# Where the third load of wo stands in SP's queue: a one-token decode block on one core

## The chip, the core and the metric

One core of a Trainium2 chip runs the kernel alone. The metric is the device time of one launch in microseconds (us). Before the change the median of three runs is 406.3 us (406.21 to 406.33).

## What is computed

One token of width 1024 goes through a layer norm and then through two branches, whose sum is added to the token:

```python
x = A_x                       # [1, 1, 1024], bf16
xn = _layernorm(x)
# branch A: attention over a cache of 65,536 keys, 32 query heads in 4 groups of 8
q = (xn @ wq).reshape(...)    # wq [1024, 4096]
scores = einsum(q, k) * 128 ** -0.5      # k_cache [1, 4, 65536, 128]
o = einsum(softmax(scores), v)           # v_cache [1, 4, 65536, 128]
A = o.reshape(1, 1, 4096) @ wo           # wo [4096, 1024]
# branch B: a two-stage MLP (with one token the shifted parts of h are all zero)
h = gelu(layernorm(xn) @ w1);  x1 = xn + shifted(h) @ w2
B = x1 + gelu(layernorm(x1) @ w3) @ w4   # w4 [3584, 1024]
out = x + A + B
```

Nearly all of the work is reading: keys and values are 64 MiB each, the weights another 34 MiB. Each byte is used once.

## The kernel before

**Slots.** Everything large is read from HBM into `slots_sb`, eight slots of 16 KB for each of the 128 partitions (2 MiB a slot). A load of keys or values takes two neighbouring slots (4 MiB), a load of `wo` one (2 MiB). The table `where` (L301) fixes the slot of each load: the last values go to slots 4 and 5 or 0 and 1 in turn (`where["v", h, j]`, L306), the last keys to 6 and 7 or 2 and 3, the four loads of `wo` to slots 2, 3, 6 and 7, and the three loads of `w4` to slots 4 and 5, then 0, then 1.

**SP's queue.** All these loads are issued by one engine, SP, in the order of the list `loads`. An issue waits, on SP, until the last users of its slot are through; whatever stands behind it on SP waits too, even where its own slot is long free. The lines are L324 (two slots), L318 (one slot: `w1`, `w2`, `wo`) and L339 (the last pieces of `w4`).

**Heads.** For each of four groups of heads the kernel reads four loads of keys, k(4h) to k(4h+3), and four of values, numbered v0 to v15 over the kernel. A load of keys is turned by VectorE (L542), multiplied on TensorE (L555), and its maximum and copy taken (L566, L567). After the fourth, `finish_head` makes the maximum of the head (L574 to L578) and the exponentials (L580, ScalarE); `transpose_p` turns these on TensorE (L589) and copies them back (L592); only then can `use_v` multiply with the values (L603). `combine` (L610 to L622) ends a head. Values run five loads behind keys (`LAG`, L627), so that after the last keys, k15, five loads of values are left: v11 of the third head and v12 to v15 of the fourth. The loads of `wo` are put in between by hand (L632).

**The end.** When v15 is used up and the head combined, the four parts of `wo` are multiplied (`use_wo`, L531, matmuls of L460), then the parts of `w4` (`use_w4`, L525, also L460). Both add into one PSUM tile; L716 adds the rest and L719 writes the output.

**What each of the last loads waits for**, besides its place in SP's queue: v12 (slots 4, 5) for v10, wo0 and wo1 (slots 2, 3) for k14, v13 (slots 0, 1) for v11, v14 (slots 4, 5) for v12, v15 (slots 0, 1) for v13, wo2 and wo3 (slots 6, 7) for k15, the first load of `w4` (slots 4, 5) for v14, the others (slots 0, 1) for v15.

The order of use on TensorE is not the order of the loads: `uses` (L626 to L640) takes keys and values in the order of the list but puts all of `wo` behind v15.

Of the kernel before, what the change touches and what calls it, by code (L numbers as in the profile page):

```python
# [163 lines left out]
def bass_parallel_sum__gqa_block_cached__mixer_s_mlp__decode_kernel(  # L164
# [37 lines left out]
    with ExitStack() as es:  # L202
# [425 lines left out]
        n_kv = 4 * HKV  # L628
        order = [("k", i) for i in range(LAG)]
        for i in range(LAG, n_kv):  # L630
            order += [("v", i - LAG), ("k", i)]
        order += [("v", n_kv - 5), ("v", n_kv - 4), ("wo", 0), ("v", n_kv - 3), ("wo", 1), ("v", n_kv - 2), ("v", n_kv - 1), ("wo", 2), ("wo", 3)]  # L632
        for kind, i in order:
            loads.append((kind,) + divmod(i, 4) if kind != "wo" else (kind, i))
            if kind != "wo":
# [119 lines left out]
```

## Time and profile before

| | |
|---|---|
| median of three runs | 406.3 us (406.21 to 406.33) |
| the profiled execution's own time | 405.76 us |
| its span, first to last instruction | 404.0 us |
| read from HBM | 169.87 MB, 420 GB/s over the span |
| VectorE busy | 183.8 us (45%) |
| TensorE busy | 154.8 us (38%) |
| ScalarE busy | 75.3 us (19%) |

The 16 DMA engines that move the data have no row among the compute engines; the line "DMA" of the slices gives their mean busy share, and "GB/s" what they moved. One slice of 40 is 10.1 us. The last loads are issued at these times (the timeline of SP; "to landing" is from the issue until all 16 engines have delivered, so issue plus this is the time of landing):

| load | issued at | us to landing | landed at |
|---|---|---|---|
| k15 (4 MiB) | 285.88 | 27.6 | 313.5 |
| v11 (4 MiB) | 287.60 | 35.6 | 323.2 |
| v12 (4 MiB) | 309.52 | 23.4 | 332.9 |
| wo0 (2 MiB) | 309.90 | 27.9 | 337.8 |
| v13 (4 MiB) | 332.04 | 15.5 | 347.5 |
| wo1 (2 MiB) | 332.42 | 20.0 | 352.4 |
| v14 (4 MiB) | 351.18 | 12.4 | 363.6 |
| v15 (4 MiB) | 352.93 | 20.5 | 373.4 |
| wo2 (2 MiB) | 353.30 | 24.9 | 378.2 |
| wo3 (2 MiB) | 353.79 | 29.3 | 383.1 |
| w4, first (4 MiB) | 367.80 | 26.2 | 394.0 |
| w4, second (2 MiB) | 375.49 | 23.4 | 398.9 |
| w4, last piece (256 KiB) | 378.05 | 23.4 | 401.5 |

### The profile page before, as it was taken

To read this page: it belongs to the slowest core of one execution; us is meant where nothing else is said; L and a number is where in the kernel's file an instruction comes from. 1 tells how busy PE (TensorE), PEld (TensorE's weight loads), DVE (VectorE), ACT (ScalarE), POOL (GpSimd) and SP (SyncE) were. 2 spreads that over 40 slices of the span, in tenths; PEclk is the share of its full clock that TensorE was granted. 3 is DMA by queue.
4 is the path that set the end of the run, shared out by engine and by line. 5 is a ranking of instruction groups with operands and counts; after the bars stand their busy time and mean duration, and the time that the engine had idled before them with its cause. 6 is when DMAs were issued, how large, how long until landed. Compare 5 with 4: busy or idle time off the path is not lost. (4 is left out here: it accounts for less than half of the span.)

```text
span 404.0 us, 3803 instructions
## 1 busy us (share of the span) xinstructions
PE 154.8 (38%) x1615; PEld 67.8 (17%) x1615; DVE 183.8 (45%) x137; ACT 75.3 (19%) x71; POOL 7.8 (2%) x38
## 2 busy tenths in 40 slices
PE   0165323244257041344561513257215152603705
PEld 0023110011023010111320101123101012301403
DVE  0135019998747263746545364748180931000200
ACT  1000000111762010191310002813010157200000
POOL 6010000000000000000000000000000000000000
PEclk9995565555556756565575565555956555666777
DMA  8999999999999999999999999999999999899995
GB/s 357 422 415 420 458 419 420 455 417 419 443 435 415 441 441 415 435 448 415 422 454 422 419 454 425 419 444 431 419 438 441 415 425 454 334 415 436 441 414 219
DMA packets 6937, 170.00 MB, mean 421 GB/s; under 512 B 904, under 2 KB 912, under 8 KB 1296
## 3 DMA queue, kind: packets, MB, share of 16 engines
q1 hardware_dynamic: 6772, 169.87, 98.3%
q8 instruction: 6, 0.10, 0.1%
q10 hardware_dynamic: 156, 0.01, 0.0%
q14 instruction: 3, 0.02, 0.0%
HBM read 169.87 MB, written 0.00 MB: 420 GB/s over the span
## 5 line engine op out<-in xcount | busy, mean ns | idle before, releaser
L542 DVE STREAM_TRANSPOSE X<-slots_sb 128x4096 f32<-128x4096 f32 x32 | 141.2, 4428 | 84.3 <-DMA slots_sb<-in_A_k_cache_dram 84.3
L555 PE MATMUL S_ps<-X,Ycur 128*32 128x512 bf16 x512 | 57.8, 596 | 139.9 <-PEq L64 126.3
L603 PE MATMUL OT_ps<-slots_sb,pT_sb 128*32 128x512 bf16 x512 | 50.9, 568 | 22.9 <-PEq L64 22.6
L567 ACT ACTIVATE S_sb<-S_ps 128x1024 f32<-128x1024 f32 x16 | 16.4, 1026 | 181.4 <-DVE mcol L566 161.4
L555 PEld LDWEIGHTS S_ps<-X,Ycur 128*32 128x32 bf16 x512 | 16.8, 124 | 176.6 <-issue 160.9
L580 ACT ACTIVATE p_sb<-S_sb,brun 128x1024 bf16<-128x1024 f32 x16 | 40.5, 2580 | 2.5 <-DVE brun L578 2.2
L603 PEld LDWEIGHTS OT_ps<-slots_sb,pT_sb 128*32 128x32 bf16 x512 | 19.9, 132 | 48.6 <-issue 46.0
L611 DVE TENSOR_TENSOR O_m<-OT_ps,selT_f 128x512 f32<-128x512 f32 x4 | 2.8, 691 | 52.1 <-PE OT_ps L603 52.1
L589 PE MATMUL PT_ps<-ident_bf,p_sb 128*128 128x128 bf16 x128 | 16.2, 307 | 18.5 <-PEq L64 18.5
L566 DVE TENSOR_REDUCE mcol<-S_ps 128x1 f32<-128x1024 f32 x16 | 19.1, 1195 | 8.6 <-PE S_ps L555 8.6
L592 ACT ACTIVATE pT_sb<-PT_ps 128x1024 bf16<-128x1024 bf16 x16 | 16.4, 1024 | 34.3 <-PE PT_ps L589 34.3
L589 PEld LDWEIGHTS PT_ps<-ident_bf,p_sb 128*128 128x128 bf16 x128 | 12.4, 138 | 24.2 <-issue 24.2
L460 PE MATMUL S_ps<-slots_sb,xn_bf 128*32 128x512 bf16 (+1 forms) x128 | 12.3, 556 | 10.4 <-DMA slots_sb<-in_B_w_dram 9.0
L460 PE MATMUL M_ps<-slots_sb,gh_bf 128*32 128x256 bf16 x112 | 5.7, 357 | 12.0 <-DMA slots_sb<-in_B_w_dram 12.0
L471 ACT ACTIVATE ge_a<-ge_b 128x8 f32<-128x8 f32 (+1 forms) x2 | 0.4, 217 | 52.2 <-DVE ge_b L470 52.2
L716 DVE TENSOR_TENSOR fin<-accr,M_ps 128x256 bf16<-128x256 f32 x1 | 0.4, 421 | 21.2 <-PE M_ps L460 21.2
L464 DVE STREAM_TRANSPOSE X<-S_ps 128x512 f32<-128x512 f32 (+1 forms) x3 | 2.6, 850 | 14.1 <-PE S_ps L460 14.1
L420 DVE CAST xP<-xP_bf 128x8 f32<-128x8 bf16 x1 | 0.2, 172 | 16.7 <-DMA xr_bf<-in_A_x_dram 16.7
L460 PEld LDWEIGHTS S_ps<-slots_sb,xn_bf 128*32 128x32 bf16 x128 | 4.5, 134 | 16.6 <-DMA slots_sb<-in_B_w_dram 9.8
L622 ACT ACTIVATE oP_bf<-cb_o 128x8 bf16<-128x8 f32 x4 | 0.8, 210 | 33.1 <-DVE cb_o L621 33.1
L460 PEld LDWEIGHTS M_ps<-slots_sb,gh_bf 128*32 128x32 bf16 x112 | 3.5, 123 | 14.2 <-DMA slots_sb<-in_B_w_dram 13.5
L434 PE MATMUL M_ps<-ln_s,ones_f 128*128 128x1 f32 x6 | 1.5, 328 | 10.6 <-DVE ln_s L433 10.6
(88 smaller groups left out, 59.1 us busy)
## 6 DMA issues: line engine op xcount, KB each, us to landing
slots_sb<-in_A_k_cache_dram SPq DMA_DIRECT2D x16, 4096.0 KB, 27.0
slots_sb<-in_A_v_cache_dram SPq DMA_DIRECT2D x16, 4096.0 KB, 26.8
slots_sb<-in_A_wq_dram SPq DMA_DIRECT2D x2, 4096.0 KB, 16.9
slots_sb<-in_A_wo_dram SPq DMA_DIRECT2D x4, 2048.0 KB, 26.4
slots_sb<-in_B_w_dram SPq DMA_DIRECT2D x2, 3584.0 KB, 32.5
slots_sb<-in_B_w_dram SPq DMA_DIRECT2D x3, 2048.0 KB, 25.9
slots_sb<-in_B_w_dram SPq DMA_DIRECT2D x1, 4096.0 KB, 26.2
slots_sb<-in_B_w_dram SPq DMA_DIRECT2D x1, 512.0 KB, 23.0
```

Of the source, the lines that this page charges most:

```text
L434: _op(q_pe, lambda e: e.matmul(M0_ps[:, c0:c0 + 1], ones_f[:, :], ln_s[:, 0:1], start=True, stop=True), reads=[b_ln, b_const], writes=[b_M0])
L460: e.matmul(out_fn(j), st_fn(kk, j), mv_fn(kk, j), start=st, stop=sp, tile_position=(0, 32 * j), skip_group_check=True))
L464: _op(q_dve, lambda e: e.transpose(out=X32[:, 1, c0:c0 + 32 * n], in_=src), reads=b_src, writes=[b_X[1]], partial=c0 > 0)
L542: turn = lambda e: e.transpose(out=X32[:, m, :], in_=K32)
L555: fns.append(lambda e, we=we, c_mid=c_mid, mv=mv: e.matmul(S_ps[bank][32 * c_mid:32 * c_mid + 32, :], Ycur[:, we, :, :].rearrange("p a g - ...
L566: _op(q_dve, lambda e: e.reduce_max(mcol[:, x:x + 1], S2, axis=AX.X), reads=[b_S[2 * i], b_S[2 * i + 1]], writes=[b_mcol], partial=x > 0)
L567: _tell(q_act, lambda e: e.activation(S_sb[:, 2 * x:2 * x + 2, :].rearrange("p s c -> p (s c)"), S2, ACTF.Copy), t_s, reads=[b_S[2 * i], b ...
L580: fn = lambda e, x=x: e.activation(p_sb[:, :, :, :, x], S_sb[:, 2 * x:2 * x + 2, :].rearrange("p s (c i) -> p s c i", i=32), ACTF.Exp, bia ...
L589: _taking(q_pe, [(t_t, 1) if c8 else (t_p, 1)], [lambda e, i=i, c=8 * c8 + i: e.transpose(out=PT_ps[:, i * P:(i + 1) * P], in_=p_sb[:, c / ...
L592: _tell(q_act, lambda e, c8=c8: e.activation(pT_sb[:, :, 32 * c8:32 * c8 + 32, :].rearrange("p a x g -> p x a g"), PT_ps[:, :].rearrange(" ...
L603: fns.append(lambda e, cl=cl, q4=q4, x0=x0: e.matmul(OT_ps[32 * q4:32 * q4 + 32, :], pT_sb[:, a, x0:x0 + 4, :].rearrange("p x g -> p (x g) ...
L611: _op(q_dve, lambda e: e.tensor_tensor(out=O_m[:, :, :], in0=OT_ps[:, :].rearrange("p (t d) -> p t d", t=4), in1=selT_f[:, :].unsqueeze(2) ...
```

## The change

In the hand-written order of the last loads, `("wo", 2)` moves from behind v14 and v15 to in front of them. Nothing is added or removed; slots, the order of use on TensorE and all other loads stay.

```diff
-        order += [("v", n_kv - 5), ("v", n_kv - 4), ("wo", 0), ("v", n_kv - 3), ("wo", 1), ("v", n_kv - 2), ("v", n_kv - 1), ("wo", 2), ("wo", 3)]
+        order += [("v", n_kv - 5), ("v", n_kv - 4), ("wo", 0), ("v", n_kv - 3), ("wo", 1), ("wo", 2), ("v", n_kv - 2), ("v", n_kv - 1), ("wo", 3)]
```

With `n_kv` = 16 the order of SP's issues at the end becomes v11, v12, wo0, v13, wo1, **wo2**, v14, v15, wo3, then the loads of `w4`.

## The prediction

> **What bounds the kernel now.** I read the page's slices and queues first, then the chain that ended last, then the timeline and SP's waits near the end.
>
> ```profile
> DMA  8999999999999999999999999999999999899995
> GB/s 357 422 415 420 458 419 420 455 417 419 443 435 415 441 441 415 435 448 415 422 454 422 419 454 425 419 444 431 419 438 441 415 425 454 334 415 436 441 414 219
> HBM read 169.87 MB, written 0.00 MB: 420 GB/s over the span
> DMA slots_sb<-in_B_w_dram 6%; PE OT_ps L603 1%; SPq L339 0%; DVE fin L716 0%; PE M_ps L460 0%
> ```
>
> The DMA engines are busy in nearly every slice while VectorE, the busiest compute engine, is at 45%. So the kernel is as long as its stream of loads, plus every moment in which the stream stands still. One slice inside stands out: the 35th (343 to 353 us) with 334 GB/s where its neighbours have 415 to 454. The chain ends in the last piece of `w4`. Next, how that slice comes about, from the timeline:
>
> ```profile
> 332.04 0.33 SPq L324 DMA_DIRECT2D slots_sb<-in_A_v_cache_dram  x1
> 332.42 0.43 SPq L318 DMA_DIRECT2D slots_sb<-in_A_wo_dram  x1
> 347.84 4.97 PE L603 MATMUL OT_ps<-slots_sb,pT_sb 128*32 128x512 bf16 x64 [1.36 <-PEq L64]
> 351.18 2.08 SPq L324 DMA_DIRECT2D slots_sb<-in_A_v_cache_dram  x2
> 353.30 0.94 SPq L318 DMA_DIRECT2D slots_sb<-in_A_wo_dram  x2
> SPq L54 <- PE OT_ps L603: 18.3, 1, 18.3
> ```
>
> SP issues v13 and wo1 at 332, then stands 18.3 us (the last line, from SP's waits) until v12 is used up at 351.18. TensorE begins v12 only at 347.84, because the exponentials and their transposes come first (L580, L589, L592, 328.5 to 347.5). Meanwhile the queue holds what v13 and wo1 left, and that is all delivered by 352.4. The windows show it run dry; a packet counts in the window in which it starts:
>
> ```profile
> 349.20:349.80 0.60, 0.60 (x12) 0.24 (x8) 0.00 (x0) 0.00 (x0) 0.00 (x0) 0.50 1.03 437
> 349.80:350.40 0.60, 0.60 (x12) 0.22 (x8) 0.00 (x0) 0.00 (x0) 0.00 (x0) 0.50 0.71 300
> 350.40:351.00 0.60, 0.60 (x16) 0.34 (x12) 0.00 (x0) 0.00 (x0) 0.00 (x0) 0.84 0.39 164
> 351.00:351.60 0.60, 0.60 (x20) 0.29 (x16) 0.00 (x0) 0.00 (x0) 0.00 (x0) 1.00 0.26 109
> 351.60:352.20 0.60, 0.60 (x16) 0.30 (x12) 0.00 (x0) 0.00 (x0) 0.00 (x0) 1.00 0.61 164
> 352.20:352.80 0.60, 0.60 (x12) 0.11 (x4) 0.00 (x0) 0.00 (x0) 0.00 (x0) 1.00 2.31 655
> 352.80:353.40 0.60, 0.01 (x3) 0.00 (x0) 0.00 (x0) 0.00 (x0) 0.00 (x0) 1.00 0.13 55
> 353.40:354.00 0.60, 0.00 (x0) 0.00 (x0) 0.00 (x0) 0.00 (x0) 0.00 (x0) 1.00 0.00 0
> 354.00:354.60 0.60, 0.00 (x0) 0.00 (x0) 0.00 (x0) 0.00 (x0) 0.00 (x0) 1.00 1.93 819
> ```
>
> The last number of a row is GB/s. 437 is 16 packets of 16 KB in 0.6 us, one for each engine. At 350.4 only 6 engines start another (164), at 351.0 only 4 (109): ten engines ran dry near 350.6, six up to 1.4 us later. v14's first packets, of 32 KB, start near 352.3, the second ones after 354. **The pause is real, but not of one length for all 16 engines.** That is the point on which the size hangs.
>
> **The change, part by part.** No instruction is added or removed: four kinds of things could move.
>
> 1. *wo2's own issue.* Slot 6 was last used by k15, whose matmuls of that half end by 320.2 (L555 at 318.26, 1.90 us); v13, ahead on SP, waits for v11's matmuls, later on TensorE. So wo2 adds no wait to SP and is issued right behind wo1, at 332.42 + 0.43, about 332.9 instead of 353.30. The issue itself is a row of 0.43 us, hidden in SP's 18.3 us wait; without that cover it would delay v14 by 0.43.
>
> 2. *The pause.* Landings (issue plus time to landing) tell the stream's pace: v13 lands 9.7 us after wo0 (347.5 - 337.8), wo1 4.9 us after v13. wo2 now keeps the stream fed 4.9 us beyond wo1: to about 355 on the early engines, 357 on the last. v14 stays at 351.18, since TensorE's work up to there touches nothing of wo2, and its first packets came 1.1 us behind its issue (352.3). So the cover is some 3 us too long, and the pause goes wholly. Its price: v14 landed 363.6 - 352.4 = 11.2 us behind wo1 where 9.7 is the pace, so 1.4 us (1.43 with the marks below) for the engine that ends last. The trace also keeps sixteen completion marks a transfer, one for each engine: wo1's lie between 350.61 and 352.45, v14's between 362.87 and 363.60. The earliest engine thus lost 12.26 - 9.72 = 2.54 us. The pause let the early ones wait and the late ones catch up.
>
> 3. *The end.* What the end gains is between these, and turns on which engines end last. In the last rows:
>
> ```profile
> 399.40:400.00 0.60, 0.60 (x24) 0.34 (x15) 0.00 (x0) 0.00 (x0) 0.00 (x0) 1.00 0.21 68
> 400.00:400.60 0.60, 0.39 (x12) 0.12 (x8) 0.00 (x0) 0.00 (x0) 0.00 (x0) 1.00 0.13 41
> q8 instruction: 1, 0.02, 3.3%
> q8 instruction: 1, 0.02, 3.5%
> ```
>
> A share of 0.13 is two engines of 16: the other 14 are done (the last piece's marks: first 399.64, fourteen by 400.3, two at 401.4 to 401.5). The two q8 lines are DMA windows of 384 to 386 and 398 to 400: in each a block of program, 16 KB, was fetched (3.3% of 16 engines over 2 us is 1.06 us on one engine). The first shows in the landings: `w4`'s first load needs 10.9 us behind wo3 (394.0 - 383.1), 1.2 over the pace. The same is how the six late engines of 350 us came about: such fetches (two of 8 KB) at 35, 69, 71, 84, 108 and 253 us, and after each the marks have one more late engine, none of them struck twice.
> Without the pause the first engine's last mark is 399.64 - 2.54 = 397.10. The six stay late to the end, the worst by 1.84: 398.94. An engine that was early and is struck late ends at 401.49 - 2.54 = 398.95 or, with the 0.3 us by which the early ones differ, up to 399.2. So the last landing moves from 401.49 to about 399.05: **2.4 us less**. Bounds: 2.54 less at best; 0.7 where the engine struck is the most belated one (it ends at 397.10 + 1.84 + 1.85, the last being the lateness of the two struck engines, so 400.8). I take the upper part, as the six fetches before the pause struck six different engines and the three behind it three.
> The Trainium skill, "DMA: Bandwidth & Descriptors", section on the anatomy of one DMA, would make a load from an empty queue cost some 2.0 us fixed plus its bytes at 436 GB/s; by that v14 would have landed 11.6 us behind its issue, at 362.8, the pause would have cost the last engine 0.6 in place of 1.4, and an estimate by it is some 0.8 less gain, 404.7. The trace has 12.4 us for the same load, so it disagrees and is used; the page's fit is for GpSimd's path.
>
> 4. *What is late next.* v14 and v15 come behind wo2: v14 lands at 352.4 + 4.9 + 9.7 = 367.1 (was 363.6), v15 at 376.8 (was 373.4). Then come v15's matmuls (3.6), the combination (377.2 to 380.9, 3.7) and `wo`'s products (96 and 32 matmuls, 2.8 + 1.1, the 96 partly beside the combination): done by 386 to 388. The cover is the wait for `w4`'s first load, 9.8 us in the profile (384.2 to 394.0); its landing moves to about 391.5, so 3 us of cover stay. If they did not, each us of lateness would cost one. `w4`'s first issue follows v14's use, 367.80 + 3.5 = 371.3, with v15 and wo3 still in the queue until 381; the pieces of L339 move likewise and stay 10 us ahead of need. No second pause.
>
> Sum: 405.76 - 2.4 = 403.4 for the profiled execution; the runs' median lies 0.5 above it (406.3), so **403.9**.
>
> **The rivals.**
>
> A. *A late fetch strikes an engine already late.* The same pause goes, but one engine ends at 400.06 to 400.8: a gain of 0.7 to 1.4, time 404.9 to 405.6, say 405.2. For it: six of 16 engines are late by then, and two fetches come; were the choice blind, over half of the cases would be so. Against: none was struck twice in either stretch.
>
> B. *It moves the pause, or wo2 is late after all* (the change does not do what it says): a wait of wo2 on something near 351, or the pause coming again at 371 before `w4`. Then 1.4 us is paid as before: 406.3. Against: the slot's users end at 320.2, and 10 us of loads stand queued at 371.
>
> C. *Slower: the pause was what kept the engines together.* With it gone lateness adds up over the whole kernel. If both late fetches strike the one engine that is 1.84 late, at 1.6 us each (1.85 less some earlier lateness), it ends at 397.10 + 1.84 + 3.2 = 402.1, 0.6 us over before: 406.9. It decides once one engine has 4.4 us of fetches on it. For it: lateness from 35 us was still there at 350. Against: fetches have gone to different engines.
>
> **How the numbers follow.** The forecast has 0.66, A 0.22, B 0.07, C 0.05. A measurement tells about 0.2%, 0.8 us, from no change. B falls under that, and the 0.02 of A with a gain under 0.8; so faster 0.66 + 0.20 = 0.86, same 0.09, slower 0.05. The range reaches from the full 2.54 with a little for the runs' spread, 403.4, to A's upper end, 405.6.
>
> **What would show it.** wo2's issue at about 332.9 and no stretch of a microsecond under 350 GB/s between 349 and 356; v14's issue still at 351.2, its landing near 367; the last landing near 399.0 with six or more engines finishing 1 to 2 us behind the rest; `w4`'s first load landing near 391.4; TensorE waiting some 3 us or more for it. Wrong would be a TensorE without that wait, a new SP wait in front of wo2, or an end near 400.5 with a single engine last (A).

## The result and the profile after

The changed kernel takes **403.38 us** (median of four runs, 403.24 to 403.39) where the kernel before takes 406.28 (406.21 to 406.33): a ratio of **0.9931**, 95% interval 0.9919 to 0.9943, or 2.9 us less. The profiled execution has 403.38 us, its span is 401.6 us (before 404.0). Of the 25 runs of the kernel before that stand beside the experiments below, one took 425.23 us, alone in a slow state, and is not compared with any other (the median of 406.19 given below is 406.17 without it).

From the page of the changed kernel, the DMA engines' slices and what was read:

```profile
DMA  8999999999999999999999999999999999999995
GB/s 359 425 416 418 460 428 419 425 455 418 416 431 457 418 418 434 454 418 418 444 444 418 421 454 431 419 428 454 421 421 431 450 410 432 421 460 421 422 414 232
HBM read 169.87 MB, written 0.00 MB: 423 GB/s over the span
```

The bytes are the same. The 35th slice has 421 GB/s instead of 334, and no slice inside stands out any more. SP's issues, from the timeline (start, duration, engine, line, tiles, count):

```profile
331.70 0.33 SPq L324 DMA_DIRECT2D slots_sb<-in_A_v_cache_dram  x1
332.08 0.90 SPq L318 DMA_DIRECT2D slots_sb<-in_A_wo_dram  x2
351.31 2.45 SPq L324 DMA_DIRECT2D slots_sb<-in_A_v_cache_dram  x2
```

Two loads of `wo` now follow v13 at 332, and v14 still goes out only at 351.3. What the DMA engines do meanwhile, in the windows (the last number is GB/s, counted by the start of each packet):

```profile
349.80:350.40 0.60, 0.60 (x12) 0.28 (x8) 0.00 (x0) 0.00 (x0) 0.00 (x0) 0.50 1.03 437
350.40:351.00 0.60, 0.60 (x9) 0.20 (x5) 0.00 (x0) 0.00 (x0) 0.00 (x0) 0.50 0.90 382
351.00:351.60 0.60, 0.60 (x12) 0.35 (x8) 0.00 (x0) 0.00 (x0) 0.00 (x0) 0.50 1.03 437
351.60:352.20 0.60, 0.60 (x16) 0.23 (x8) 0.00 (x0) 0.00 (x0) 0.00 (x0) 0.80 0.90 382
352.20:352.80 0.60, 0.60 (x20) 0.32 (x12) 0.00 (x0) 0.00 (x0) 0.00 (x0) 1.00 1.02 437
352.80:353.40 0.60, 0.52 (x12) 0.02 (x4) 0.00 (x0) 0.00 (x0) 0.00 (x0) 1.00 1.03 437
353.40:354.00 0.60, 0.00 (x0) 0.00 (x0) 0.00 (x0) 0.00 (x0) 0.00 (x0) 1.00 0.90 382
```

382 and 437 are 14 and 16 packets of 16 KB in 0.6 us: all engines go on without a break, where before they went from 300 down to 109 between 349.8 and 351.6. The end, in the same view:

```profile
396.40:397.00 0.60, 0.54 (x12) 0.44 (x16) 0.00 (x0) 0.00 (x0) 0.00 (x0) 0.50 0.81 297
397.00:397.60 0.60, 0.60 (x20) 0.44 (x16) 0.00 (x0) 0.00 (x0) 0.00 (x0) 0.50 0.50 181
397.60:398.20 0.60, 0.60 (x20) 0.44 (x16) 0.00 (x0) 0.00 (x0) 0.00 (x0) 0.50 0.39 143
398.20:398.80 0.60, 0.60 (x16) 0.24 (x8) 0.00 (x0) 0.00 (x0) 0.00 (x0) 0.50 0.06 20
```

A DMA share of 0.50 and 0.39 is about half of the 16 engines, in a stretch in which the others are done. Before, it was two engines of 16 that came last. The marks of the last piece say the same: before, fourteen lie between 399.64 and 400.4 and two at 401.4 to 401.5; now seven lie between 397.14 and 397.4 and nine between 397.7 and 398.99. The last landing moved from 401.49 to 398.99 us, by 2.50. The span became only 2.38 shorter, because the last four products, behind that landing, took 0.29 us before (granted clock 1.00 in that window) and 0.41 now (0.50).

### The profile page after: what moved, and what is told of

It reads as the page before. It is cut to its first block, busy times and chain, and to the rows that moved or that the text cites. A ratio compares the mean times of both kernels' runs of the same rounds, so it can differ in the third digit from the quotient of the medians.

```text
span 401.6 us, 3803 instructions
## 1 busy us (share of the span) xinstructions
PE 151.8 (38%) x1615; PEld 65.7 (16%) x1615; DVE 183.7 (46%) x137; ACT 75.3 (19%) x71; POOL 7.7 (2%) x38
## 5 line engine op out<-in xcount | busy, mean ns | idle before, releaser
L589 PE MATMUL PT_ps<-ident_bf,p_sb 128*128 128x128 bf16 x128 | 14.8, 287 | 19.0 <-PEq L64 19.0
L589 PEld LDWEIGHTS PT_ps<-ident_bf,p_sb 128*128 128x128 bf16 x128 | 11.2, 129 | 24.2 <-issue 24.2
L615 PE MATMUL M_ps<-O_L,selL 128*128 128x129 f32 x8 | 2.8, 444 | 8.1 <-PEq L64 8.1
```

Of the source, the lines that this page charges most:

```text
L589: _taking(q_pe, [(t_t, 1) if c8 else (t_p, 1)], [lambda e, i=i, c=8 * c8 + i: e.transpose(out=PT_ps[:, i * P:(i + 1) * P], in_=p_sb[:, c / ...
L615: _taking(q_pe, [(t_o, 1)], [lambda e: e.matmul(M0_ps[:, 256:257 + P], selL[:, :, :].rearrange("p g x -> p (g x)"), O_L[:, :], start=True, ...
```

## The experiments

Times are medians; the kernel before was run beside each group of kernels on the same chip (406.19 beside the first, 406.15 beside the second). "Lateness" is by how much a completion mark of a transfer lies behind the first of its sixteen marks. The marks carry no name of an engine; which mark belongs to the same engine in the next transfer is read from the distances, which hardly change from one transfer to the next.

### The kernel before, a second profile

No edit.

> The kernel before, unchanged, for a second profile. The theory (the pause near 350 us has a price that depends on how late each DMA engine is, and blocks of program fetched by a DMA engine make it late): the same pause, issue of v14 near 351, v14 landing some 11.2 us behind wo1; a span between 404.0 and 404.6, since the timed runs lie 0.5 above the profiled one, and where it is longer, the excess lies in a late landing and not in the pause. Rival (the first profile was short by chance in the pause): the difference lies between wo1's and v14's landing.

Measured: 406.14 us, span 404.4. The pause is there again: wo1 lands at 352.4 and v14 at 363.8, 11.4 us behind it. The span is 0.38 longer than in the first profile, and most of that lies **in the pause**: v14 was issued at 351.43 instead of 351.18 and the last landing came at 401.75 instead of 401.49. The other 0.1 lies behind the last landing: the last four products took 0.40 us at a granted clock of 0.50, where the first profile has 0.29 at 1.00. On this point the expectation was wrong and its rival right. Between these two profiles of the old order, a quarter of a microsecond on TensorE's way to v12 is a quarter of a microsecond at the end. The lateness of the engines in the marks has the same form: ten engines within 0.2 us and six at 1.0 to 1.7 for wo1, then 0.7 at most for v14.

### A quarter of wo2 in front of v14

```diff
+            if h == 4:
+                view = slots_sb[:, i, 0:Q4]
+                _dma(q_sp, ch_q, lambda e, view=view, src=src: e.dma_start(out=view, in_=src[:, 0:Q4]), writes=[slots[i].buf])
+                return []
...
-        order += [("v", n_kv - 5), ("v", n_kv - 4), ("wo", 0), ("v", n_kv - 3), ("wo", 1), ("v", n_kv - 2), ("v", n_kv - 1), ("wo", 2), ("wo", 3)]
+        order += [("v", n_kv - 5), ("v", n_kv - 4), ("wo", 0), ("v", n_kv - 3), ("wo", 1), ("wo", 4), ("v", n_kv - 2), ("v", n_kv - 1), ("wo", 2), ("wo", 3)]
```

`("wo", 4)` is the first quarter of wo2 (`Q4` is a quarter of a slot); `("wo", 2)` here loads the other three, so SP has one issue more.

> The kernel before with only a quarter of wo2 (512 KiB, 1.2 us of the stream) in front of v14; the other three quarters stay behind v15. Theory (every DMA engine idles from its own last byte until v14's first one, so each us of queued bytes saves one us): 1.2 us less than before, 405.1 (404.8 to 405.4), v14 landing 10.0 or so behind the quarter's landing. Rival one (a queue that runs dry costs one fixed price, and any queued load avoids it): 403.4, as with all of wo2. Rival two (the gain comes from wo2 being on chip earlier for the end): 406.3, since most of wo2 is as late as before.

Measured: 405.25 us (nine runs, 405.03 to 405.38), ratio 0.9978 (0.9968 to 0.9988), 0.94 less than before. Its windows:

```profile
350.40:351.00 0.60, 0.60 (x12) 0.30 (x8) 0.00 (x0) 0.00 (x0) 0.00 (x0) 0.50 0.89 369
351.00:351.60 0.60, 0.60 (x9) 0.18 (x4) 0.00 (x0) 0.00 (x0) 0.00 (x0) 0.50 1.00 410
351.60:352.20 0.60, 0.60 (x12) 0.34 (x8) 0.00 (x0) 0.00 (x0) 0.00 (x0) 0.50 0.38 150
352.20:352.80 0.60, 0.60 (x12) 0.21 (x7) 0.00 (x0) 0.00 (x0) 0.00 (x0) 0.50 1.77 519
352.80:353.40 0.60, 0.60 (x12) 0.30 (x8) 0.00 (x0) 0.00 (x0) 0.00 (x0) 0.72 1.21 437
353.40:354.00 0.60, 0.60 (x16) 0.11 (x4) 0.00 (x0) 0.00 (x0) 0.00 (x0) 1.00 0.29 109
```

The stream runs on until 351.6 where it had thinned out before 350.4, and then thins all the same (150, later 109). Of the three readings only the theory's fits: neither one price for the whole pause (403.4) nor nothing (406.3). v14 lands 10.5 us behind the quarter, so 0.8 over the pace of 9.7 instead of 1.4 (1.7 in the second profile of the kernel before). That 0.94 came and not 1.2 goes with two things in this trace: v14 was issued later (351.52, where the two profiles before have 351.18 and 351.43), and the shorter pause lined the engines up less (lateness of v14 up to 1.2 instead of 0.7). How much each of the two took is not separated.

### wo2 and wo3 both in front of v14

```diff
-        order += [("v", n_kv - 5), ("v", n_kv - 4), ("wo", 0), ("v", n_kv - 3), ("wo", 1), ("v", n_kv - 2), ("v", n_kv - 1), ("wo", 2), ("wo", 3)]
+        order += [("v", n_kv - 5), ("v", n_kv - 4), ("wo", 0), ("v", n_kv - 3), ("wo", 1), ("wo", 2), ("wo", 3), ("v", n_kv - 2), ("v", n_kv - 1)]
```

> wo2 and wo3 both in front of v14 and v15. Theory: wo2 alone covers the pause with some us to spare, so nothing more is won: 403.4 (403.1 to 403.9). v14 and v15 land 4.9 us later than in the changed kernel (371.8 and 381.5), TensorE's wait of 3.4 us for the first load of w4 goes to nothing, and its products with w4 begin up to 2 us later than 391.5, which the next wait (2.5 us, for the second load of w4) still hides. Rival two (the gain comes from wo being on chip earlier): a further gain of 1 us or more. Slower than 404.2 would say that the spare time behind v15 is smaller than read.

Measured: 403.31 us (403.28 to 403.46), ratio 0.993 (0.9912 to 0.9948): the changed kernel's time. What TensorE does at the end (timeline):

```profile
387.90 5.34 PE L460 MATMUL M_ps<-slots_sb,oP_bf 128*32 128x256 bf16 x128 [0.19 <-issue]
393.06 2.26 PE L460 MATMUL M_ps<-slots_sb,gh_bf 128*32 128x256 bf16 x64
396.38 1.06 PE L460 MATMUL M_ps<-slots_sb,gh_bf 128*32 128x256 bf16 x32 [1.05 <-DMA slots_sb<-in_B_w_dram]
```

The products with `w4` start at 393.06 with no wait in front of them, 1.7 us after their load landed (391.4): the spare time of the changed kernel, 3.4 us, is used up. The next wait, 1.05 us, takes the rest. More cover than the pause needs buys nothing, and wo3 lying ready earlier is worth nothing.

### wo1 behind v14 as well

```diff
-        order += [("v", n_kv - 5), ("v", n_kv - 4), ("wo", 0), ("v", n_kv - 3), ("wo", 1), ("v", n_kv - 2), ("v", n_kv - 1), ("wo", 2), ("wo", 3)]
+        order += [("v", n_kv - 5), ("v", n_kv - 4), ("wo", 0), ("v", n_kv - 3), ("v", n_kv - 2), ("v", n_kv - 1), ("wo", 1), ("wo", 2), ("wo", 3)]
```

> wo1 too behind v14 and v15, so that the queue runs dry 4.9 us sooner than in the kernel before. Theory: every engine idles 4.9 us more, 406.3 + 4.9 = 411.2 (410.8 to 411.7); v14 issued at 351 as before and landing near 363.5. Rival one (a fixed price for each pause): 406.3, as before.

Measured: 411.16 us (411.11 to 411.45), ratio 1.0124 (1.0106 to 1.0142): 4.97 more for 4.9 us of stream less in the queue. The windows have an empty stretch of six microseconds (the rows between 347 and 351, left out here, have a share of 0.00 too):

```profile
345.00:346.00 1.00, 0.55 (x6) 0.58 (x7) 0.00 (x0) 0.31 (x1) 0.00 (x0) 0.50 0.39 164
346.00:347.00 1.00, 0.47 (x5) 0.20 (x2) 0.00 (x0) 0.50 (x1) 0.00 (x0) 0.50 0.00 0
...
351.00:352.00 1.00, 1.00 (x13) 0.36 (x8) 0.00 (x0) 0.00 (x0) 0.00 (x0) 0.50 0.00 0
352.00:353.00 1.00, 1.00 (x20) 0.52 (x16) 0.00 (x0) 0.00 (x0) 0.00 (x0) 0.88 1.65 459
```

v14 lands at 363.7, as before (363.6 and 363.8), and the stream behind it is longer by wo1's 4.9 us. Nothing behind the pause makes up for it.

### The changed kernel, a second profile

No edit.

> The changed kernel once more, for a second profile: span 401.5 to 401.7, last landing near 399.0, and again six or more DMA engines that finish 1 to 2 us behind the rest. If lateness came from something accidental, it would lie on other engines and at other times in this profile; by the theory it grows at the same blocks of program as before (near 34, 69, 71, 84, 108 and 253 us).

Measured: 403.32 us, span 401.6, last landing 398.94. Blocks of program are fetched at 35, 69, 72, 85, 108 and 253 us again, and the lateness has the same form (ten marks within 0.4 us for wo2, six at 0.9 to 1.9). v14 was issued at 351.59, 0.28 later than in the first profile of this kernel, and the end did not move.

### Shorter products at the end, in both orders

Of the products with `wo` and `w4` only the first row of each load or piece is computed; loads and waits stay.

```diff
-                rows_mv(k, d_parts(view, 0), lambda kk, t: at_border(gh_bf[:, :], grp * R + kk, t), b_gh, bu, [b_M1],
+                rows_mv(1, d_parts(view, 0), lambda kk, t: at_border(gh_bf[:, :], grp * R + kk, t), b_gh, bu, [b_M1],
...
-            rows_mv(R, d_parts(view, 0), lambda kk, t: at_border(oP_bf[:, h, :], kk, t), b_oP[h], b, [b_M1], False, False)
+            rows_mv(1, d_parts(view, 0), lambda kk, t: at_border(oP_bf[:, h, :], kk, t), b_oP[h], b, [b_M1], False, False)
```

> The order of loads of the kernel before; of the products with wo and w4 only the first row of each load or piece is computed (20 matmuls for w4 in place of 112, 16 for wo in place of 128), so that TensorE's program is some 400 instructions shorter at its end and the blocks of program fetched near 385 and 398 us should not be needed, or one of them. All loads and their waits stay. Theory (in the old order the pause lines the engines up, and what then makes the end late is an engine struck by such a late fetch): without the late fetches the last landing comes some 1.1 us earlier, 405.2; with one of them left the same as before. Rival one (the pause has one price for all, fetches cost nothing): 406.3 less at most 0.2 for the shorter matmuls behind the last landing.

Measured: 405.14 us (nine runs, 404.92 to 405.32), ratio 0.9975 (0.9965 to 0.9985): 1.0 less than the kernel before. Of these two lines, the first is the only row of its queues from 375 to 400 us. The second stands in the kernel before for the same stretch, beside the row of its loads, and is two packets of program:

```profile
q1 hardware_dynamic: 938, 10.48, 98.9%
q8 instruction: 2, 0.03, 0.5%
```

The last window in which a load still runs, and the last load in the chain that ended last (start, duration), both of the shortened kernel:

```profile
400.00:400.60 0.60, 0.34 (x8) 0.11 (x4) 0.00 (x0) 0.00 (x0) 0.00 (x0) 0.50 0.04 14
378.45 22.40 DMA slots_sb<-in_B_w_dram
```

At 400.0 to 400.6 the share is 0.04 where the kernel before has 0.13: the two last engines are gone, and the last mark is at 400.86, 0.9 behind the first, instead of 1.85. A third block, of 8 KB, is still fetched at 371.5, before the stretch shown; the last mark of v14 lies 0.56 behind the first, that of v15 0.95, and this one late engine stays the last to the end.

> The same shortened products in the changed order. Theory: here the end is set as well by the engines that were struck early and stay late to the end, so taking the late fetches away gains nothing but the shorter last matmuls: 403.4 (403.0 to 403.5), and the difference between the two orders falls from 2.9 to some 1.5 to 2.0. Rival one: the same difference of 2.9 between the two orders as with the whole products.

Measured: 403.32 us (403.25 to 403.45), ratio 0.9932 (0.9919 to 0.9946): 0.06 less than the changed kernel's four runs, and the same as the run of its second profile. The two late fetches are gone here too, and the last mark still lies 1.9 behind the first (397.20 and 399.06), since the engines struck before 350 us are still late. The queues from 375 to 400 us and the last load:

```profile
q1 hardware_dynamic: 861, 9.31, 88.1%
381.38 17.68 DMA slots_sb<-in_B_w_dram
```

The two orders now differ by 1.8 us instead of 2.9. So these two late fetches cost 1.0 us in the old order and nothing that can be told from the noise in the new one, as the theory had it; fetches without a price would have left the difference alone.

## Why the prediction was right

- **wo2's own issue.** Predicted at about 332.9 without a wait. It is the second of the two issues at 332.08 (0.90 us for both), in SP's long wait, which still ends with v12's use: v14 goes out at 351.31 (predicted "still at 351.2").
- **The pause goes wholly, with time to spare.** Shown by the windows of the changed kernel, and by the spare time: wo2 and wo3 together give no more than wo2 alone, a quarter of it gives 0.94, and taking wo1's 4.9 us away costs 4.97.
- **The size at the end.** The step said that the engine that ends last had lost only 1.43 us to the pause and the earliest 2.54, and that the end gains nearly the larger of these because the early-struck engines (398.94) and the late-struck ones (398.95 to 399.2) then end together. Predicted last landing 399.05, measured 398.99. Read from the distances, the early-struck ones end by 398.72 (they were 1.67 late and not 1.84 in this profile) and the two late-struck ones at 398.88 and 398.99; without those, in the shortened kernel, the early-struck ones end at 399.06 (they were 1.94 late there). The reason is shown from both sides: without the last two fetches the old order ends at 400.86, the new one at 399.06, 1.8 apart and no longer 2.5. Of these 1.8 the last engine lost 1.47 to the pause (v14 lands 11.19 us behind wo1 in that trace, where the pace is 9.72), near the predicted 1.43. The rest is about what the 8 KB fetch at 371.5 added: it left one engine 0.9 behind the first at the end, where the pause had left 0.56 at most.
- **What is late next.** Predicted landings: v14 367.1, v15 376.8, first load of `w4` about 391.4. Measured 366.9 (issue 351.31 plus 15.6), 376.6 and 391.5. TensorE waits 3.4 us for that last one, predicted "some 3 us or more":

```profile
391.53 2.44 PE L460 MATMUL M_ps<-slots_sb,gh_bf 128*32 128x256 bf16 x64 [3.40 <-DMA slots_sb<-in_B_w_dram]
```

- **The half microsecond that was missed.** For the profiled execution the sum gave 403.4, and it took 403.38. The forecast of 403.9 added 0.5, by which the runs before lay over their profiled execution, as though that were part of every run. It was not: **the term mis-sized is that offset**, 0.5 forecast and 0.0 measured. The two profiles of the kernel before differ by 0.38 us of span, 0.26 by when v14 was issued and 0.11 by the granted clock of the last four products; the two of the changed kernel differ by 0.28 in that issue and not in their span. In the four profiles with a full queue (the changed kernel twice, wo2 and wo3 both in front, the shortened one) v14 is issued between 351.31 and 351.71, and the last landing lies between 398.91 and 399.06, not in the same order. The pause handed TensorE's timing on to the end; a full queue didn't. In the runs beside the experiments the kernel before spreads from 405.7 to 406.5 but for the one named above, the changed kernel over all its runs from 403.24 to 403.39; that this spread has the same cause is likely but not shown, as the unprofiled runs have no issue times.
- **The rivals.** A (a late fetch on an engine already late) did not come: the last mark lies 1.85 behind the first in both profiles of the changed kernel, about the lateness that wo1 had already (1.67 and 1.93), and not twice that. Nine marks of the last piece are late (0.6 to 1.85), after nine fetches behind the 30th microsecond. B is excluded by the issue times. C would need one engine struck three times; no mark shows one struck twice. Which engine a fetch takes isn't in the trace, which gives packets without their engine; that the engines struck are different ones is read from the count of late marks alone, and why they are different stays open.

The Trainium skill, "DMA: Bandwidth & Descriptors", section on queues, rings and completion order, says that a DMA engine takes turns, packet by packet, between the queues that have work for it. Its section on why a DMA increments its semaphore by 16 and not by 1 says that only the full count of 16 means that all data has landed. The trace is in keeping with both, though it shows no engine taking turns: a 16 KB packet of program takes 0.9 to 1.1 us, and in the old order one mark of the `w4` load behind it lies 1.86 us after the first, where none did by more than 0.71 for wo3, so that the load lands 1.2 us over the pace.

## What to carry to other kernels

Where the stream of loads is the bound, look for the window in which it thins out, ask which load at the head of the queue waits for a compute engine, and put enough ready bytes in front of it. Here 1.2 us of them saved 0.94, 4.9 us taken away cost 4.97, and beyond the length of the pause more of them saved nothing. Work out the gain on the engine that ends last and not as a mean, because a pause also lines up engines that had drifted apart. Here the full queue had a second benefit: the end no longer followed the timing of the compute engines.

## What was not expected of the hardware

A block of program fetched while the queue is full makes one of the 16 DMA engines late, and that lateness stays for hundreds of microseconds: in the changed kernel six engines are 0.8 to 1.7 us late at 350 us, after six fetches between 34 and 253 us, and the last mark is 1.85 us late at the end. Only the dry queue took most of it away (from 1.84 to 0.73 us in the kernel before). Taking the program's last two blocks away was worth 1.0 us in the order with the pause and 0.06 in the order without; for the six early ones the cause is read from the times alone.

An engine falls back by more than the packet of program takes. In the kernel before, the 8 KB packet at 253 us took 0.31 us, and one mark went from 0.47 to 1.14 us behind the first; the 16 KB packet at 35 us took 1.03 us, and one mark went to 1.77 where none had been more than 0.50 behind. Why it is more isn't shown.
